# A due-time table for the planner, late decode from the first layer, and the last pair's values in another PSUM slot

## The chip, the cores and the metric

One core of one Trainium2 chip runs the whole program. The metric is the device time of one launch in microseconds (us). The kernel before took 1105.01 us, the median of three runs (1103.29, 1105.01 and 1106.9). The profiled execution, from which all rows below come, took 1104.88 us itself, of which 1103.1 us is the span that the profiler shows.

## The reference, cut to what matters

```
q, k, v: [4, 12, 448, 64]                      # batch, heads, sequence, head size
scores = q @ k.T / 8 - log(448)
x      = sigmoid(scores) @ v                    # -> [4 * 448 tokens, 768]
h      = x @ w_in                               # 768 x 2048
x      = (h - tanh(h)) @ w_out                  # 2048 x 768
gate   = sigmoid(x @ w_gate)                    # 768 x 1536
out    = (gate * (x @ w_val)) @ w_out2          # 1536 x 768
```

All of it is in float32. The kernel keeps the precision by splitting each operand into a rounded high part and a low rest and by adding three products (high with high, high with low, low with high).

## The kernel before

**Attention.** 24 head pairs p are worked one after another. For each pair TensorE makes scores `sa` and `sl` (L310, L322), ScalarE makes sigmoids `at` and `al` of them (L314, L326), and one pair later `values(p)` multiplies these with v into a PSUM tile (L338, L345), which VectorE or ScalarE copies to `x` (L353). PSUM has three slots that matter here: tag `px` holds scores (the third scores slot), tag `pv` holds the values of a pair and has one buffer. So the values of pair 23 can't begin before the copies of pair 22 have emptied `pv`.

**First layer.** 32 steps i, that is 8 groups of 256 hidden columns by 4 batches t. `hidden_mm` (L361) makes the hidden PSUM tile `ph`, a chain of ScalarE and VectorE instructions makes `h - tanh(h)` from it (`u`, `mk`, `s1`, `s2`, `y`, L395 to L434; `g` is its high part on ScalarE, L431, then its low part on VectorE, L434), and `project_group` (L468) multiplies `g` with w_out into `po`, which L481 or L585 adds to the accumulators `acc`.

**Second layer.** 12 blocks k in two passes of six (`NBLK`): a pass is one half of the batches, a block 256 of the 1536 hidden columns. A block multiplies by a Strassen scheme: seven products (`TERMS` = a11, s1, s2, a12, s3, s4, a22) with the gate weights n = 3k, then seven with the value weights n = 3k+1 (`product`, L999, into banks `pa`, `pb`, `pc`, `pe`). Copies on ScalarE (L1012) move a bank's partial sum into the next bank. `prepare` makes the operands of a pass: sums of accumulators (L629, VectorE), their highs (L762, ScalarE), their lows (L768, VectorE). `divide(n)` splits the weights: high on ScalarE (L842), lows (L853) on GpSimd, for n = 0, 1, 2 and 18 also on VectorE. `finish` makes gate times value: high `gg` on ScalarE (L1059), lows (L1064) on GpSimd, in the last block on VectorE too. The output projection of a block, 12 groups `pq` (L468), is put among the products of the next block as `fillers`, and VectorE adds each group to the output accumulator (L479, L481). Before the first block the join to layer 1 has the last groups `po31` as fillers.

**What sets the order.** All instructions are written out by a program that plans. Each piece of ScalarE, VectorE and GpSimd work is a `Task` with a due time. `spend(t, ...)` stands after each piece of TensorE work: it moves a clock `now` on by t and issues those tasks, by due time, that fit in the spare room of each engine; `must` issues one at once. Each engine and each DMA queue then works strictly in the order of issue. Fillers are placed by tables: `SHARE0` puts all 12 twelfths after s2 in block 0, `SHARE` spreads them over s2, a12, s3, s4 and a22 of the gate half, and `SHARE_END` puts those of block 5 into its value half. Operands of the second pass are planned from block 5 on (`prepare(1)`). The late decode of packed weights (`mq`: ScalarE L145, VectorE L148 to L163, written out by SyncE's queue and read back as `mm`) is planned when layer 1 has been issued.

## Time and profile before

| what | value |
|---|---|
| median of three runs | 1105.01 us |
| profiled execution, own time | 1104.88 us |
| its span | 1103.1 us |
| TensorE (PE) busy | 1084.3 us, 98% of the span, 6085 matmuls |
| VectorE (DVE) busy | 809.3 us, 73% |
| ScalarE (ACT) busy | 617.7 us, 56% |
| GpSimd (POOL) busy | 427.4 us, 39% |
| chain that ended last | PE 93%, DVE 3%, ACT 2%, POOL 1%, issue 1% |

The busy time of TensorE includes stretches at a lower clock, where each matmul takes longer. The granted clock (PEclk) stands at 1.00 in most stretches; where it stands below, a part of the stretch ran at the lower of the two levels (1.2 instead of 2.4 GHz). An instruction's idle time in square brackets is the time that its engine waited just before it, with what ended the wait.

### The profile page before, as it was taken

The numbers are of one execution on the slowest core, as the hardware profiler recorded it, in microseconds if no ns is written. First come the engines' busy times: TensorE is split into PE (matmuls) and PEld (weight loads), VectorE is DVE, ScalarE is ACT, GpSimd is POOL, SyncE is SP. The second block draws the span as 40 slices with busy tenths as digits, with TensorE's granted clock in tenths as the row PEclk, the third lists the DMA queues.
The fourth block names the chain that finished last, engine by engine and source line by source line (L and its number), as shares of the span: only waits on it lengthen the run. The fifth ranks groups of instructions, "written<-read, shape, count | busy, mean of one in ns | idle before, by whom it ended". The sixth has DMA issues, their size and how long they took to land.

```text
span 1103.1 us, 15973 instructions
## 1 busy us (share of the span) xinstructions
PE 1084.3 (98%) x6085; PEld 974.2 (88%) x6085; DVE 809.3 (73%) x1112; ACT 617.7 (56%) x861; POOL 427.4 (39%) x432
## 2 busy tenths in 40 slices
PE   9999989999999999999999999999998999999998
PEld 6677779999999999999998889999997999999997
DVE  4778647899998989899977879996669453443334
ACT  6878745577777777777767444444354334333320
POOL 5455300011111111111136357586598445546531
PEclk9999999999999999999999899999999999999999
DMA  7666302324343434244320136455212311201202
GB/s 202 191 189 188 122 1 86 101 89 128 100 143 100 144 100 141 87 129 133 113 72 29 58 132 224 159 187 172 88 42 70 136 68 58 83 32 58 87 1 100
DMA packets 40205, 119.80 MB, mean 109 GB/s; under 512 B 6080, under 2 KB 21440, under 8 KB 40128
## 3 DMA queue, kind: packets, MB, share of 16 engines
q1 hardware_dynamic: 36896, 116.38, 32.8%
q0 software_dynamic: 3072, 2.17, 0.9%
q8 instruction: 48, 0.79, 0.3%
q10 hardware_dynamic: 160, 0.23, 0.1%
q14 instruction: 29, 0.24, 0.1%
HBM read 99.09 MB, written 19.66 MB: 108 GB/s over the span
## 4 chain that ended last, share of the span: by engine, by line
PE 93%; DVE 3%; ACT 2%; POOL 1%; issue 1%; DMA 0%; SPq 0%; ACTq 0%; POOLq 0%
PE ph L361 21%; PE po L468 21%; PE pq L468 15%; PE pa L999 8%; PE pc L999 7%; PE pb L999 7%; PE pv L345 5%; PE sa L310 4%; PE pe L999 3%; PE sl L322 1%; PE pv L338 1%; DMA st<-in_w_in_dram 0%; PE pz L1173 0%; ACT at L314 0%; POOL gg L1064 0%
## 5 line engine op out<-in xcount | busy, mean ns | idle before, releaser
L468 PE MATMUL po<-g,w 128*128 128x448 f32 x1152 | 240.0, 366 | 2.1 <-ACT g L431 1.6
L361 PE MATMUL ph<-x,w 128*128 128x448 f32 x1152 | 235.8, 362 | 0.2 <-ACT at L314 0.2
L468 PEld LDWEIGHTS po<-g,w 128*128 128x128 f32 x1152 | 216.0, 189 | 21.0 <-ACT g L431 1.9
L361 PEld LDWEIGHTS ph<-x,w 128*128 128x128 f32 x1152 | 215.8, 187 | 15.3 <-ACT at L314 0.6
L178 POOL TENSOR_TENSOR w<-m,w 128x384 fp32r<-128x384 f32 x64 | 63.6, 1016 | 380.9 <-issue 299.0
L468 PE MATMUL pq<-gg,w 128*128 128x448 f32 x864 | 184.4, 364 | 5.1 <-POOL gg L1064 3.5
L468 PEld LDWEIGHTS pq<-gg,w 128*128 128x128 f32 x864 | 162.5, 188 | 17.8 <-POOL gg L1064 4.5
L853 POOL TENSOR_TENSOR w_t<-mm,w_t 128x384 fp32r<-128x384 f32 x90 | 96.8, 1105 | 137.9 <-ACT w_t L842 137.5
L481 DVE TENSOR_TENSOR acco<-pq,acco 128x448 f32<-128x448 f32 x120 | 73.8, 620 | 71.5 <-PE pq L468 70.6
L999 PE MATMUL pa<-a,w_b 128*128 128x448 f32 x432 | 94.6, 363 | 0.0
L999 PEld LDWEIGHTS pa<-a,w_b 128*128 128x128 f32 x432 | 81.5, 189 | 5.6
L314 ACT ACTIVATE at<-sa,bias_s 128x896 f32<-128x896 f32 x72 | 67.3, 1008 | 8.1 <-PE sa L310 8.0
L481 DVE TENSOR_TENSOR acc<-po,acc 128x448 f32<-128x448 f32 x90 | 55.4, 617 | 14.0 <-PE po L468 13.9
L853 POOL TENSOR_TENSOR w_b<-mm,w_b 128x384 fp32r<-128x384 f32 x54 | 59.8, 1128 | 15.0 <-ACT w_b L842 13.3
L1064 POOL TENSOR_TENSOR gg<-sg,gg 128x448 fp32r<-128x448 f32 x42 | 55.1, 1341 | 24.4 <-ACT gg L1059 24.4
L398 ACT ACTIVATE y<-ph 128x896 f32<-128x896 f32 x32 | 29.4, 919 | 59.2 <-PE ph L361 59.0
L345 PE MATMUL pv<-at,vt 128*64 128x224 f32 x576 | 60.8, 361 | 0.0
L145 ACT ACTIVATE m<-st 128x768 f32<-128x768 f32 x32 | 29.0, 908 | 56.5 <-POOL w L178 55.0
L345 PEld LDWEIGHTS pv<-at,vt 128*64 128x64 f32 x576 | 39.8, 139 | 19.7 <-issue 8.3
L842 ACT ACTIVATE w_t<-mm 128x768 fp32r<-128x768 f32 x48 | 39.3, 838 | 30.0 <-DVE mm L879 26.9
L853 POOL TENSOR_TENSOR w<-mm,w 128x384 fp32r<-128x384 f32 x44 | 47.1, 1094 | 21.3 <-ACT w L842 20.7
L310 PE MATMUL sa<-sp 64*128 64x448 f32 x432 | 51.1, 376 | 0.2 <-ACT at L314 0.2
(113 smaller groups left out, 1858.8 us busy)
## 6 DMA issues: line engine op xcount, KB each, us to landing
mm<-kept SPq DMA_DIRECT2D x36, 768.0 KB, 4.2
st<-in_w_out_dram SPq DMA_DIRECT2D x28, 768.0 KB, 4.9
st<-in_w_in_dram SPq DMA_DIRECT2D x16, 768.0 KB, 4.3
st<-in_w_gate_dram SPq DMA_DIRECT2D x12, 768.0 KB, 5.0
st<-in_w_val_dram SPq DMA_DIRECT2D x12, 768.0 KB, 4.9
kept<-mk SPq DMA_DIRECT2D x22, 384.0 KB, 5.6
kt<-in_k_dram SPq DMA_DIRECT2D x48, 112.0 KB, 3.8
kept<-mq SPq DMA_DIRECT2D x14, 384.0 KB, 5.5
```

Of the source, the lines that this page charges most:

```text
L178: (low or nc.gpsimd).tensor_tensor(out=w1[:, r], in0=mf[:, r], in1=w0[:, r].bitcast(F32), op=ALU.subtract)
L310: nc.tensor.matmul(pa[:, j, :S], kk[r, ki, c], qq[r, qi], start=(i == 0), stop=(i == 2),)
L314: nc.scalar.activation(out=at[:, :, c], in_=pa[:, :, :S], func=AF.Sigmoid, bias=bias_s, scale=qk_scale,)
L345: nc.tensor.matmul(po[j * D:(j + 1) * D, h, :SH], vt[:, j, c], at[:, j, c, h * SH:(h + 1) * SH], start=False, stop=(c == NCH - 2),)
L361: nc.tensor.matmul(o, w(i), xv(j), start=first and n == 0, stop=last and n == 2, skip_group_check=seeded,)
L398: nc.scalar.activation(out=y, in_=h, func=AF.Tanh)
L468: nc.tensor.matmul(po[:, :S], w[:, a, d], gt[:, c, j], start=n == 0 and not seeded, stop=n == last, skip_group_check=seeded,)
L481: nc.vector.tensor_tensor(out=at[:, d], in0=po[:, :S], in1=at[:, d], op=ALU.add)
L842: nc.scalar.activation(out=w0, in_=quarters(lo, hi), func=AF.Copy)
L853: eng.tensor_tensor(out=w1[:, r], in0=quarters(lo, hi)[:, r], in1=w0[:, r].bitcast(F32), op=ALU.subtract,)
L999: nc.tensor.matmul(bank[term], w[:, i, half * KH + c], t[:, j, c], start=fresh and at == 0, stop=at == 3 * KH - 1, skip_group_check=not fresh,
L1064: eng.tensor_tensor(out=gt[t][:, 1, j], in0=sg[t][:, j], in1=gt[t][:, 0, j].bitcast(F32), op=ALU.subtract,)
```

## The change

It does these things. A table `TUNE` gives an offset in us to the due time of each task. It also holds the arguments of some `spend` calls (`e0` to `e9`), a slightly smaller spare (1.94 for 2.0), flags `v{n}` and `u{k}` that let the lows of weights n and of block k's gates go to VectorE as well as to GpSimd, and for each block a plan `f{k}`: how many fillers stand after each of its 14 products. Operands of the second pass are planned from block 4 on (`early`), not from block 5, and all sums of that pass may begin at once then. The late decode is registered inside the first layer, at its step `TAIL2` = 28. The values of the last pair go to tag `px`. In the attention's last steps the first instructions of layer 1's chain for step 0 are issued in another order, and its last ones after `values(23)`. The matmuls are the same in number; the lines of the changed kernel are 36 to 42 higher than those of before.

```
+TUNE = {
+    "c28": 11.1, "c29": 1.4, "c30": -5.1, "d20": -2.4, "d21": 2.2, "d22": 6.6, "d23": 3.4,
...
+    "f0": [0, 0, 4, 0, 0, 0, 2, 0, 0, 0, 0, 0, 0, 0],
...
-        po = psx.tile([128, 2, 512], F32, tag="pv", name=f"pv{p}")
+        po = psx.tile(
+            [128, 2, 512], F32, tag="px" if p == NP - 1 else "pv", name=f"pv{p}"
+        )
...
-            spend(1.2)
+            spend(1.2, TUNE.get("e4", 0.9), TUNE.get("e5", 1.0))
...
-    SPARE = 2.0
+    SPARE = TUNE.get("spare", 2.0)
...
             self.haste = False
+            due += TUNE.get(name, 0.0)
...
-            kinds = dict(v=0.6, g=1.3) if FLEX or n in (0, 1, 2, 18) else dict(g=1.3)
+            kinds = dict(v=0.6, g=1.3) if TUNE.get(f"v{n}", n in (0, 1, 2, 18)) else dict(g=1.3)
...
-                task.add(dict(v=0.7, g=1.4) if FLEX or k == NK - 1 else dict(g=1.4), f, [h])
+                task.add(dict(v=0.7, g=1.4) if TUNE.get(f"u{k}", k == NK - 1) else dict(g=1.4), f, [h])
...
-        for term in TERMS:
+        plan = TUNE.get(f"f{k}", PLAN_END if k == NBLK - 1 else PLAN0 if k == 0 else PLAN)
+
+        def fill(at):
+            for _ in range(plan[at]):
+                if fillers:
+                    fillers.pop(0)()
+
+        for at, term in enumerate(TERMS):
             product(3 * k, term)
             gate(term)
-            if not after:
-                fill(share.get(term, 0))
+            fill(at)
...
-                run(act)
-                for f in dve[:3]:
+                for f in (act[1], act[0], act[2], dve[0], dve[1]):
                     f()
...
+            first = NPRE - len(early) // 4
+            late_u.append(NU1 + first)
+            st_at[NU1 + first] = 0.0
+            for j in range(first, NPRE):
+                decoding(j, min(begin_of(j // 2) - 16.0, begin_of(3 * NBLK - 3)))
...
-            if k == NBLK - 1:
+            if k == TUNE.get("early", NBLK - 2):
                 for term in TERMS:
                     x_free.setdefault((1, term), None)
-                x_free[1, "a11"] = 0.0
-                for term in ("s1", "s2", "s3", "s4"):
-                    x_free[1, "sum" + term] = 0.0
+                x_free[1, "a11"] = x_free[1, "sums1"] = x_free[1, "sums2"] = 0.0
+                x_free[1, "sums4"] = x_free[1, "sums3"] = 0.0
                 prepare(1, begin_of(3 * NBLK) - 4.0, free1)
```

Of the flags, `u11` is false, so the last block's gate lows, which could go to VectorE, now go to GpSimd alone: VectorE and GpSimd had two each, and now GpSimd has all four. Counted over the program, 26 lows of weights and 14 lows of gates move from GpSimd to VectorE (28 to 54 and 2 to 16). Between the first block and the fifth (blocks 1 to 4) VectorE gets 14 instructions more.

ScalarE at the join of layer 1 to block 0, before (`s2_0` is the high of the operand s2 of pass 0, `room` the copy of bank `pe`, `g31` the high of the last step of layer 1):

```order
L585 ACTIVATE acc2_2224<-po30_5_5761 128x448
L407 ACTIVATE s231_5705<-mk31_5703,gb_92 128x896
L1012 ACTIVATE pb0_5787<-pa0_5786 128x448
L762 ACTIVATE s2_0_5812<-acc0_1996 128x1344
L1012 ACTIVATE room_5783<-pe0_5789 128x448
L762 ACTIVATE s4_0_5831<-acc1_2110 128x1344
L1012 ACTIVATE pc0_5788<-pb0_5787 128x448
L431 ACTIVATE g31_5700<-y31_5702 128x896
```

The same place on ScalarE in the changed kernel:

```order
L623 ACTIVATE acc2_2224<-po30_5_5764 128x448
L1054 ACTIVATE pb0_5790<-pa0_5789 128x448
L445 ACTIVATE s231_5709<-mk31_5707,gb_92 128x896
L1054 ACTIVATE room_5786<-pe0_5792 128x448
L801 ACTIVATE s2_0_5822<-acc0_1996 128x1344
L801 ACTIVATE a22_0_5838<-acc1_2110 128x1344
L1054 ACTIVATE pc0_5791<-pb0_5790 128x448
L469 ACTIVATE g31_5704<-y31_5706 128x896
```

The copies out of `pa0` and `pe0` now stand ahead of `s2_0`, and a22's high in the place of s4's.

VectorE at the same join, before (`ph31` and `y31` are the chain of the last step of layer 1):

```order
L418 SCALAR_TENSOR_TENSOR ph31_5647<-s131_5704,ph31_5647 128x2x448
L423 SCALAR_TENSOR_TENSOR ph31_5647<-s231_5705,ph31_5647 128x2x448
L768 TENSOR_TENSOR s2_0_5812<-acc0_1996,s2_0_5812 128x448 x3
L428 COPY_PREDICATED y31_5702<-mk31_5703,ph31_5647 128x896
L629 TENSOR_TENSOR acc0_1996<-acc1_2110,acc0_1996 128x448 x2
L434 TENSOR_TENSOR g31_5700<-y31_5702,g31_5700 128x896
```

And in the changed kernel (`mq` and `st54` are the late decode):

```order
L456 SCALAR_TENSOR_TENSOR ph31_5651<-s131_5708,ph31_5651 128x2x448
L193 SCALAR_TENSOR_TENSOR mq_5462<-st54_5346,mq_5462 128x768
L199 SCALAR_TENSOR_TENSOR mq_5462<-st54_5346,mq_5462 128x768
L807 TENSOR_TENSOR s2_0_5822<-acc0_1996,s2_0_5822 128x448 x3
L461 SCALAR_TENSOR_TENSOR ph31_5651<-s231_5709,ph31_5651 128x2x448
L466 COPY_PREDICATED y31_5706<-mk31_5707,ph31_5651 128x896
L472 TENSOR_TENSOR g31_5704<-y31_5706,g31_5704 128x896
```

Two decode instructions come in ahead of s2's lows, the chain's step L423 moves behind these lows, and the sums L629 leave the place between the chain's last two steps.

ScalarE where the second pass begins (block 6), before (`gg5_0` and `gg5_1` are the gate highs of block 5, of which block 6's fillers need the lows; `p56_0` is the copy of bank `pe`):

```order
L842 ACTIVATE w17_0_7690<-mm17_7591 128x768
L762 ACTIVATE s4_1_7726<-acc3_2346 128x1344
L762 ACTIVATE a22_1_7738<-acc3_2346 128x1344
L762 ACTIVATE s3_1_7750<-acc2_2224 128x1344
L842 ACTIVATE w17_1_7776<-mm17_7591 128x768
L1012 ACTIVATE pb6_7761<-pa6_7760 128x448
L1059 ACTIVATE gg5_0_7416<-sg5_0_7414 128x896
L1059 ACTIVATE gg5_1_7417<-sg5_1_7415 128x896
L1012 ACTIVATE p56_0_7759<-pe6_7763 128x448
```

And in the changed kernel:

```order
L881 ACTIVATE w17_0_7698<-mm17_7591 128x768
L801 ACTIVATE a22_1_7724<-acc3_2346 128x1344
L1101 ACTIVATE gg5_0_7425<-sg5_0_7423 128x896
L881 ACTIVATE w17_1_7748<-mm17_7591 128x768
L881 ACTIVATE w19_b1_7753<-mm19_7713 128x768
L1054 ACTIVATE pb6_7762<-pa6_7761 128x448
L801 ACTIVATE s4_1_7791<-acc3_2346 128x1344
L1054 ACTIVATE p56_0_7760<-pe6_7764 128x448
L801 ACTIVATE s3_1_7804<-acc2_2224 128x1344
```

`gg5_0` moves ahead of the copy of `pa6`, and the highs of s4 and s3 move behind it. On TensorE the fillers of block 5 stand behind the product a12 of block 6 (4 after a12, 1 after s3, 5 after s4, 1 each after s1 and a12 of the value half), where before two stood behind s2 and two behind a12.

## Rows read from the trace of the kernel before

**Rows 1.** The page's first part: busy time, share of the span, instructions.

```profile
PE 1084.3 (98%) x6085; PEld 974.2 (88%) x6085; DVE 809.3 (73%) x1112; ACT 617.7 (56%) x861; POOL 427.4 (39%) x432
```

**Rows 2.** Stretches: length, busy of PE, PEld, DVE, ACT, POOL; PEclk, DMA, GB/s.

```profile
132.00:152.00 20.00, 16.93 (x123) 12.26 (x120) 9.38 (x10) 10.11 (x13) 1.99 (x2) 0.91 0.12 41
...
592.00:615.00 23.00, 20.04 (x80) 16.42 (x79) 20.24 (x23) 15.76 (x21) 14.17 (x11) 0.85 0.21 69
...
660.00:810.00 150.00, 150.00 (x751) 140.59 (x751) 117.51 (x151) 65.58 (x99) 105.21 (x86) 1.00 0.47 156
...
830.00:860.00 30.00, 25.38 (x116) 22.68 (x116) 26.95 (x36) 11.64 (x15) 19.87 (x16) 0.94 0.24 84
```

**Rows 3.** Timeline of PE, attention's end: start, length, operation, [idle before].

```profile
141.50 0.61 PE L338 MATMUL pv<-al,vt 64*64 64x224 f32 x8
142.04 2.49 PE L345 MATMUL pv<-at,vt 128*64 128x224 f32 x24
147.41 1.02 PE L338 MATMUL pv<-al,vt 64*64 64x224 f32 x8 [2.88 <-DVE x L353]
148.36 3.55 PE L345 MATMUL pv<-at,vt 128*64 128x224 f32 x24
```

**Rows 4.** Timeline of ACT, the last reader of the px slot.

```profile
134.82 0.64 ACT L326 ACTIVATE al<-sl,bias_s 128x448 f32<-128x448 f32 x1
```

**Rows 5.** Timeline of PE, join of layer 1 to block 0.

```profile
601.76 1.97 PE L999 MATMUL pe<-s,w_t 128*128 128x448 f32 x9
...
606.51 0.47 PE L999 MATMUL pb<-s,w_t 128*128 128x448 f32 x1 [0.80 <-DVE s L768]
608.58 3.86 PE L468 MATMUL po<-g,w 128*128 128x448 f32 x8 [1.60 <-ACT g L431]
...
646.12 2.08 PE L468 MATMUL pq<-gg,w 128*128 128x448 f32 x9 [1.12 <-DVE w L853]
```

**Rows 6.** Timeline of ACT, the same join.

```profile
602.46 1.32 ACT L762 ACTIVATE s<-acc 128x1344 fp32r<-128x1344 f32 x1
603.76 0.54 ACT L1012 ACTIVATE room<-pe 128x448 f32<-128x448 f32 x1
...
607.58 0.95 ACT L431 ACTIVATE g<-y 128x896 fp32r<-128x896 f32 x1
```

**Rows 7.** Timeline of DVE, the same join.

```profile
602.01 1.10 DVE L423 SCALAR_TENSOR_TENSOR ph<-s,ph 128x896 f32<-128x896 f32 x1
603.81 2.65 DVE L768 TENSOR_TENSOR s<-acc,s 128x448 fp32r<-128x448 f32 x3 [0.70 <-ACT s L762]
606.38 1.17 DVE L428 COPY_PREDICATED y<-mk,ph 128x896 f32<-128x896 int32 x1
...
609.45 1.08 DVE L434 TENSOR_TENSOR g<-y,g 128x896 fp32r<-128x896 f32 x1
```

**Rows 8.** Timeline of PE, start of the second pass.

```profile
843.96 2.08 PE L999 MATMUL pb<-s,w_t 128*128 128x448 f32 x9 [1.78 <-ACT pb L1012]
...
848.68 0.47 PE L468 MATMUL pq<-gg,w 128*128 128x448 f32 x1 [1.85 <-POOL gg L1064]
850.15 2.88 PE L468 MATMUL pq<-gg,w 128*128 128x448 f32 x7 [0.99 <-POOL gg L1064]
```

**Rows 9.** Timeline of PE, then of POOL, the last block's projection.

```profile
1085.45 0.88 PE L468 MATMUL pq<-gg,w 128*128 128x448 f32 x3 [0.61 <-POOL gg L1064]
...
1083.86 3.04 POOL L1064 TENSOR_TENSOR gg<-sg,gg 128x448 fp32r<-128x448 f32 x2 [12.27 <-ACT gg L1059]
```

**Rows 10.** Timeline of DVE (three rows), then of POOL beside the last two.

```profile
617.64 0.54 DVE L853 TENSOR_TENSOR w_b<-mm,w_b 128x384 fp32r<-128x384 f32 x1
...
782.03 0.62 DVE L481 TENSOR_TENSOR acco<-pq,acco 128x448 f32<-128x448 f32 x1 [0.26 <-PE pq L468]
782.58 1.38 DVE L853 TENSOR_TENSOR w_b<-mm,w_b 128x384 fp32r<-128x384 f32 x1
...
781.55 1.99 POOL L853 TENSOR_TENSOR w_b<-mm,w_b 128x384 fp32r<-128x384 f32 x2
```

More of the change, by code (lines that the diff above doesn't have):

```diff
@@ L29 @@
 GGAP = 24
+TUNE = {
[32 rows of a table added]
+}
 @with_exitstack
@@ L1004, in product @@
                     at += 1
-            spend(1.8, 0.2 if term == "s3" else 0.9, 0.4 if term in ("a11", "s2") else 0.8)
+            spend(
+                1.8, TUNE.get("e0", 0.2) if term == "s3" else TUNE.get("e1", 0.9),
+                TUNE.get("e2", 0.4) if term in ("a11", "s2") else TUNE.get("e3", 0.8),
+            )
             if LAST.get(term) == key:
@@ L1088, in value @@
                 finish(1, join(sg[1][:, 0], pc, sg[1][:, 0], ALU.mult))
-        share = SHARE0 if k == 0 else SHARE
-        after = SHARE_END if k == NBLK - 1 else {}
-        total = len(fillers)
-        def fill(part):
-            while len(fillers) > total - total * part // 12:
-                fillers.pop(0)()
-        for term in TERMS:
+        plan = TUNE.get(f"f{k}", PLAN_END if k == NBLK - 1 else PLAN0 if k == 0 else PLAN)
[4 more added lines that the diff above has]
+        for at, term in enumerate(TERMS):
             product(3 * k, term)
             gate(term)
-            if not after:
-                fill(share.get(term, 0))
+            fill(at)
         if k:
             p5.append(mp[0].tile([128, S], F32, tag="p5", name=f"p5{k}_1"))
-        for term in TERMS:
+        for at, term in enumerate(TERMS):
             product(3 * k + 1, term)
@@ L1109, in block @@
             value(term)
-            fill(after.get(term, 0))
+            fill(7 + at)
+        while fillers:
+            fillers.pop(0)()
         g_t["b", k] = gt
-    SHARE0 = dict(s2=12)
-    SHARE = dict(s2=2, a12=4, s3=7, s4=10, a22=12)
-    SHARE_END = dict(a11=2, s1=4, s2=6, a12=8, s3=10, s4=12)
+    PLAN0 = [0, 0, 6] + [0] * 11
+    PLAN = [0, 0, 2, 2, 3, 3, 2] + [0] * 7
+    PLAN_END = [0] * 7 + [2] * 6 + [0]
     g_task = {}
@@ L1141, in run @@
                         box["po"] = seed(f"pq{k}_{t}_{d + 1}", at, d + 1)
-                    spend(1.2)
+                    spend(1.2, TUNE.get("e6", 0.9), TUNE.get("e7", 1.0))
                     if by_act and d % 2:
@@ L1206 @@
         assert not todo
-        for f in dve[3:]:
+        for f in (act[3], act[4], dve[2], dve[3], dve[4]):
             f()
         values(NP - 1)
+        for f in dve[5:]:
+            f()
         att_ctx.close()
@@ L1254 @@
                 busy["v"] = max(busy["v"], now[0])
-                spend(7.2)
+                spend(7.2, TUNE.get("e8", 0.9), TUNE.get("e9", 1.0))
                 if i > TAIL2:
@@ L1284 @@
         last_chain.append(chain)
-        first = NPRE - len(early) // 4
-        late_u.append(NU1 + first)
-        st_at[NU1 + first] = 0.0
-        for j in range(first, NPRE):
-            decoding(j, min(begin_of(j // 2) - 16.0, begin_of(3 * NBLK - 3)))
         fillers = list(groups1(N1 - 1))
```

30 rows, old and new, of the table TUNE are left out of this document.

## The prediction, made before the changed kernel ran

> **What bounds the kernel now.** I read the page's first part, then the stretches, then in the stretches that lose time the timeline of TensorE, and from each of its waits the timeline of the engine named there. The first shows TensorE busy for 1084.3 of 1103.1 us [rows 1]. The stretches tell what busy means: from 660 to 810 us it ran 751 matmuls in 150.00 us, 0.200 us each, at a clock of 1.00 [rows 2]. That is the floor, and the matmuls are the same in number after the change; only time over 0.200 us a matmul can go. By this price the stretch 592 to 615 loses 23.0 - 80 x 0.2 = 7.0 us and the stretch 830 to 860 loses 30.0 - 116 x 0.2 = 6.8 us, both at a mean granted clock under 1.00 [rows 2]. So a wait there costs twice: its own length, and matmuls at 1.2 GHz in place of 2.4 GHz behind it. The end of attention, 132 to 152, is the third such stretch [rows 2].
>
> **Place 1, the last pair's values in the px slot.** TensorE waits 2.88 us ahead of the values of pair 23, until VectorE has emptied the slot of pair 22. These values then take from 147.41 to 151.91 = 4.50 us, the same work for pair 22 from 141.50 to 144.53 = 3.03 us [rows 3]: the wait has left the clock low. The px slot was last read at 134.82 + 0.64 = 135.46 [rows 4], six us before it is wanted now. The values of pair 23 would then begin at 144.53, at the high clock, and end at 147.56, not 151.91: **-4.35**. What could be late next is the chain of layer 1's step 0, since the copies out of pair 23's slot stand ahead of its last instructions now; but those copies move up by the same 4 us. I take no cost, and up to +1 for a new wait there.
>
> **Place 2, the join of layer 1 to block 0.** Before, ScalarE makes the high of s2 at 602.46 and copies bank pe afterwards [rows 6]. Now the copy stands first, and pe's matmuls end at 601.76 + 1.97 = 603.73 [rows 5]. So the copy runs from 603.75 to 604.3, the high takes 1.32 to 605.6 [rows 6], and VectorE's three lows 2.65 to 608.2 [rows 7]. The two decode instructions ahead of these lows cost nothing: no row here has them, but at the 1.10 of the nearest VectorE row [rows 7] they need 2.2 us, and VectorE has from 603.1 until 605.6. Behind the lows now come the chain's step L423 (1.10), L428 (1.17), ScalarE's g (0.95) and VectorE's low of g (1.08) [rows 6, 7]: 608.2 + 4.3 = 612.5, less some 0.1 of overlap at each of the joints. Before, that low ended at 609.45 + 1.08 = 610.53 [rows 7]. The sums that stood between the last two steps are gone, which is in this count. That is +1.9. If GpSimd is idle then, the three lows take about 0.54 each, as the one low without a neighbour did [rows 10], not 0.88, and +0.9 is left; I take +1.5. TensorE's wait of 1.12 for a weight low at 646.12 [rows 5] goes, since weights 2 and 3 may now be split by either engine and the plan brings no fillers before s2: -1.1. Sum of the place **+0.4**, with bounds of -3 (the waits of 0.80 and 1.60 us [rows 5] and half the clock loss go) and +3 (none of the 1.1 comes, and the longer wait keeps the clock low for another 1.5).
>
> **Place 3, start of the second pass.** TensorE waits 1.78 us for the copy of pa, then 1.85 and 0.99 for the lows of block 5's gates [rows 8], and the rest of the 6.8 is low clock. Three things change. Sums and a high for the second pass are made in block 4 already. The copy no longer waits behind three highs of 1.3 each, but behind one, a gate high of 0.95 and two weight highs; how much earlier it starts depends on when those weights have landed, so I keep the 1.78 whole. And gate 0's high stands ahead of the copy, its lows may go to VectorE, and the product a12 stands ahead of the first filler, which gives the lows 9 x 0.2 = 1.8 us more. The two waits for gates, 2.84 in sum, should go, and with them the low clock: 6.8 - 1.8 = **-5.0**. Bounds: -6.8, if the copy is early too, and 0, if VectorE is as late with the lows as GpSimd.
>
> **What the lows on VectorE cost.** 40 lows move to VectorE. A low with nothing beside it on GpSimd takes 0.54 us, one beside GpSimd 1.38 [rows 10]. At 1.38, 14 instructions more in the steady stretch bring VectorE from 117.51 to 136.8 of 150 us [rows 2]: it still fits, and TensorE, busy for the whole of that stretch, hides it. I take 0; if the cover goes, see the third rival.
>
> The Trainium skill, "SBUF — State Buffer", section "Who interferes with whom", says that a VectorE instruction with two inputs in SBUF and a GpSimd instruction take a shared pair of ports in turn, and that one with at most one SBUF input does not contend. The trace agrees on both sides: 1.38 against 0.54 for the low, which has two such inputs, and 0.62 for the evacuation L481 beside GpSimd, which reads one operand from PSUM [rows 10]. By this rule moving a low wins no throughput, only a place in another queue, so it bears on the second rival, and it speaks against the third.
>
> **Tail.** The last block's gate 0 had one low on VectorE and one on GpSimd; now GpSimd has both, ahead of both of gate 1. GpSimd took 3.04 us for two [rows 9], so the second ends at 1083.86 + 3.04 = 1086.90, and the sixth matmul, which ran at 1085.45 + 0.2 = 1085.65 [rows 9], waits for it: **+1.3**. Bounds 0 (VectorE was running beside GpSimd, without it GpSimd may take half) and +1.5.
>
> **Other edits.** The fill plans, the offsets and the decode in the first layer move work that stands beside a TensorE which loses nothing: 150.00 of 150.00 us in the long stretch of layer 2 [rows 2]. I take 0, from -0.5 (less DMA crowding) to +3 (one new wait of 1.5 with its clock).
>
> **Sum.** -4.35 + 0.4 - 5.0 + 1.3 = -7.65 against the profiled execution's own 1104.88 (its span of 1103.1 and 1.8 around it): 1097.2. The median of the three runs is 1105.01, 0.1 from it, so I forecast 1097.
>
> **Rivals.**
> 1. *Clean recovery.* At place 3 the copy is early as well (-6.8), the tail costs nothing, and place 2 loses only the 1.1: 1104.9 - 4.35 - 6.8 - 1.1 = 1092.6. For it: ScalarE is half idle, with 65.58 busy of 150 in the steady stretch, so an early copy is a matter of order alone [rows 2]. Against it: at place 2 the order moves the s2 high later.
> 2. *Gains given back on the port.* Lows on VectorE at 1.38 keep TensorE waiting at places 2 and 3 as GpSimd did: 2.84 of wait and the low clock stay, and only place 1 with the tail's cost, less some of the 1.1, is won: 1104.9 - 4.35 + 1.3 - 0.5 = 1101.3. For it: VectorE is at 26.95 of 30 us in 830 to 860 [rows 2]. Against it: the order of ScalarE there changes apart from the port.
> 3. *VectorE's queue becomes the bound, and the kernel slower.* VectorE works in order, so each moved low stands ahead of an evacuation of the output projection. A low and an evacuation take 1.38 + 0.62 = 2.0 us [rows 10], while TensorE makes a group of six matmuls in 1.2: 0.8 late, when no free bank takes it up. With half of the 40 lows badly placed that is 16 us: 1097 + 16 = 1113. It decides from some 10 lows on, which eat up the 7.65. For it: VectorE is the fullest engine beside TensorE. Against it: 0.00 lost in 150 us with 117.51 busy [rows 2].
> 4. *The slot is not free.* Another tile or a due time holds the px slot, or the chain of step 0 makes TensorE wait as long: place 1 wins nothing, the rest stays: 1104.9 + 0.4 - 5.0 + 1.3 = 1101.6. Against it: the 135.46 above.
>
> **How the numbers follow.** A run of this kernel tells from no change what is over 0.3%, 3.3 us: faster is under 1101.7, slower over 1108.3. Forecast 0.50 (its own range 1093.5 to 1100.5), clean recovery 0.21, port 0.15, slower 0.08, slot 0.06. Faster: 0.49 + 0.21 + about two thirds of the 0.21 of rivals 2 and 4 = 0.83; same: the other third and a little of the forecast's tail, 0.10; slower 0.07. The range leaves out the slower rival and the lower end of clean recovery: 1090.5 to 1102.5.
>
> **What would show it.** Place 1: no wait ahead of pair 23's values, and layer 1 beginning behind them about 4.4 us earlier. Place 2: g's low of the last step about 1.5 us later against the start of block 0, and no wait for weight 2's low. Place 3: in the first product of block 6 a wait of 1.8 or less for the copy, none for the gates, clock 1.00. Tail: a wait of some 1.3 more in the last block's first group. It is wrong if VectorE's busy share in blocks 1 to 4 nears 150 of 150 with waits of TensorE for evacuations, or if new waits stand in the blocks where none were.

## The result and the profile after

The changed kernel takes **1092.88 us** (median of 4 runs, 1092.74 to 1094.55), against 1104.95 for the kernel before on the same chip: a ratio of 0.989, with a 95% interval of 0.9875 to 0.9912. The profiled execution took 1092.74 us with a span of 1091.0, so 12.1 us went out of the span. 1097 was forecast, with a range of 1090.5 to 1102.5.

First the same views as [rows 1] and [rows 2]: the page's first part, and the stretches (length, busy time of PE, PEld, DVE, ACT and POOL with their instructions, PEclk, DMA share, GB/s).

```profile
PE 1078.5 (99%) x6085; PEld 971.6 (89%) x6085; DVE 822.6 (75%) x1153; ACT 617.8 (57%) x861; POOL 384.9 (35%) x391
```

```profile
132.00:152.00 20.00, 19.81 (x143) 15.76 (x142) 9.88 (x11) 10.73 (x13) 1.99 (x2) 1.00 0.12 41
...
592.00:615.00 23.00, 18.29 (x80) 15.54 (x79) 19.10 (x26) 14.25 (x18) 10.62 (x9) 0.93 0.34 117
...
660.00:810.00 150.00, 150.00 (x752) 140.61 (x750) 119.46 (x162) 64.85 (x99) 84.94 (x69) 1.00 0.44 140
...
830.00:860.00 30.00, 30.00 (x151) 28.12 (x150) 26.25 (x36) 13.19 (x20) 22.73 (x18) 1.00 0.35 128
```

TensorE runs the same 6085 matmuls and is busy 5.8 us less, because fewer of them run at the low clock. The first and the last stretch now hold 143 and 151 matmuls where 123 and 116 stood. The join, 592 to 615, still holds 80. VectorE did not fill up: 119.46 of 150 us, 2 us more than before with 11 instructions more.

Where the time came from is read from the start of the same product in both traces. Each row gives how much earlier it starts now, and the difference to the row ahead.

| product | earlier by, us | step, us | what stands there |
|---|---|---|---|
| layer 1, next matmul behind pair 23's values | 4.45 | -4.45 | place 1 |
| block 0, a11 | 4.73 | -0.28 | a ScalarE wait of 0.21 in layer 1 gone |
| block 0, a11 of the value half | 4.03 | +0.70 | the join |
| behind block 1's fillers | 5.43 | -1.40 | wait for weight 2's low |
| block 6, a11 | 5.61 | -0.18 | in block 5 a product of 1.98 us where 1.80 is usual gone |
| block 6, s3 of the gate half | 12.64 | -7.03 | place 3 |
| end | 12.10 | +0.54 | tail |

**Place 1.** TensorE at the end of attention (start, length, operation; a wait would stand in brackets):

```profile
144.97 2.49 PE L383 MATMUL pv<-at,vt 128*64 128x224 f32 x24
147.39 5.88 PE L399 MATMUL ph<-x,w 128*128 128x448 f32 x28
```

The 2.88 us ahead of pair 23's values [rows 3] are gone, its 24 matmuls take 2.49, as pair 22's did before [rows 3], and layer 1 follows at 147.39 without a wait.

**Place 2.** At the join TensorE waits longer than before, 1.84 and 2.73 us against 0.80 and 1.60 [rows 5]:

```profile
595.23 1.96 PE L1038 MATMUL pa<-a,w_b 128*128 128x448 f32 x9
...
600.83 2.21 PE L1038 MATMUL pb<-s,w_t 128*128 128x448 f32 x9 [1.84 <-ACT s L801]
605.77 6.97 PE L506 MATMUL po<-g,w 128*128 128x448 f32 x24 [2.73 <-ACT g L469]
612.58 1.96 PE L1038 MATMUL pa<-a,w_b 128*128 128x448 f32 x9
```

ScalarE and VectorE there, to be set against [rows 6] and [rows 7]:

```profile
599.02 0.54 ACT L1054 ACTIVATE room<-pe 128x448 f32<-128x448 f32 x1 [0.26 <-PE pe L1038]
...
604.76 0.95 ACT L469 ACTIVATE g<-y 128x896 fp32r<-128x896 f32 x1 [1.16 <-DVE y L466]
```

```profile
600.81 1.70 DVE L807 TENSOR_TENSOR s<-acc,s 128x448 fp32r<-128x448 f32 x3 [1.79 <-ACT s L801]
...
605.75 1.09 DVE L472 TENSOR_TENSOR g<-y,g 128x896 fp32r<-128x896 f32 x1 [1.02 <-ACT g L469]
```

The order is the one that the prediction went through: copy, high, three lows, then the chain to g. The three lows take 1.70 us, not 2.65. For the same stretch the trace of before has, on TensorE:

```profile
599.96 1.96 PE L999 MATMUL pa<-a,w_b 128*128 128x448 f32 x9
...
608.58 10.61 PE L468 MATMUL po<-g,w 128*128 128x448 f32 x36 [1.60 <-ACT g L431]
619.03 1.96 PE L999 MATMUL pa<-a,w_b 128*128 128x448 f32 x9
```

Before, 27 + 36 = 63 matmuls took 619.03 - 599.96 = 19.07 us; at 0.2 each that is 12.6, and 6.47 are lost, 2.40 of them in waits and 4.07 to the low clock. Now 27 + 24 = 51 take 612.58 - 595.23 = 17.35 us, and 7.15 are lost, 4.57 in waits and 2.58 to the clock. (The other 12 matmuls run later. What is put down to the clock holds, at each wait, also the 0.16 us or so in which the matmul ahead of it ends: nine matmuls in a row take 1.96 us by the rows, and the next begins 1.80 after their start.) So the waits grew by 2.17 and the join by 0.7.

The longer of the two waits is for ScalarE's high of g, before and after. Counted from the start of block 0, that high ended at 607.58 + 0.95 - 599.96 = 8.57 us before [rows 6], and ends at 604.76 + 0.95 - 595.23 = 10.48 now, 1.91 later.

**Weight 2's low.** The wait of 1.12 us in block 1 [rows 5] is gone. ScalarE makes weight 2's two highs in the changed kernel ahead of block 1, where before the second of them came 4.4 us into it (block 1 begins at 634.80 now and began at 638.83). The line of before stands first:

```profile
643.27 0.84 ACT L842 ACTIVATE w<-mm 128x768 fp32r<-128x768 f32 x1
...
630.68 1.56 ACT L881 ACTIVATE w<-mm 128x768 fp32r<-128x768 f32 x2
```

**Place 3.** TensorE, ScalarE and GpSimd at the start of the second pass, to be set against [rows 8]:

```profile
836.40 1.96 PE L1038 MATMUL pb<-s,w_t 128*128 128x448 f32 x9
838.20 1.96 PE L1038 MATMUL pa<-a,w_b 128*128 128x448 f32 x9
840.00 4.96 PE L506 MATMUL pq<-gg,w 128*128 128x448 f32 x24
```

```profile
831.36 0.95 ACT L1101 ACTIVATE gg<-sg 128x896 fp32r<-128x896 f32 x1 [1.22 <-DVE sg L1070]
...
834.80 0.53 ACT L1054 ACTIVATE pb<-pa 128x448 f32<-128x448 f32 x1 [1.02 <-PE pa L1038]
```

```profile
833.72 1.47 POOL L667 TENSOR_TENSOR acc<-acc 128x448 f32<-128x448 f32 x1
835.15 2.97 POOL L1106 TENSOR_TENSOR gg<-sg,gg 128x448 fp32r<-128x448 f32 x2
```

The three waits are gone. ScalarE stood idle for 1.02 us until TensorE had ended pa, and then made the copy at once. The high of gate 0 was made 3.4 us ahead of that copy, and its two lows, still on GpSimd, end at 835.15 + 2.97 = 838.12, ahead of the fillers at 840.00.

**Tail.** TensorE in the last block's projection, to be set against [rows 9]:

```profile
1072.43 0.47 PE L506 MATMUL pq<-gg,w 128*128 128x448 f32 x1 [0.22 <-POOL gg L1106]
1073.52 13.68 PE L506 MATMUL pq<-gg,w 128*128 128x448 f32 x67 [0.62 <-POOL gg L1106]
```

GpSimd now makes all four lows, and takes 4.47 us for the four:

```profile
1071.22 4.47 POOL L1106 TENSOR_TENSOR gg<-sg,gg 128x448 fp32r<-128x448 f32 x4 [13.26 <-ACT gg L1101]
```

That is 1.12 each, and TensorE waits 0.22 and then 0.62 us for them, where it waited 0.61 before.

### The profile page after: what moved, and what is told of

Read it like the earlier page. It is cut to its first block, busy times and chain, and to the rows that moved or that the text cites. A ratio compares the mean times of both kernels' runs of the same rounds, so it can differ in the third digit from the quotient of the medians.

```text
span 1091.0 us, 15944 instructions
## 1 busy us (share of the span) xinstructions
PE 1078.5 (99%) x6085; PEld 971.6 (89%) x6085; DVE 822.6 (75%) x1153; ACT 617.8 (57%) x861; POOL 384.9 (35%) x391
## 3 DMA queue, kind: packets, MB, share of 16 engines
q0 software_dynamic: 3072, 2.17, 0.9%
## 4 chain that ended last, share of the span: by engine, by line
PE 96%; ACT 1%; DMA 1%; DVE 1%; POOL 0%; issue 0%; SPq 0%; ACTq 0%; DVEq 0%; POOLq 0%
PE ph L399 21%; PE po L506 21%; PE pq L506 16%; PE pa L1038 8%; PE pc L1038 8%; PE pb L1038 8%; PE pv L383 5%; PE pe L1038 4%; PE sa L346 4%; PE sl L358 1%; PE pv L376 1%; DMA st<-in_w_in_dram 0%; ACT at L350 0%; DMA kt<-in_k_dram 0%; POOL gg L1106 0%
## 5 line engine op out<-in xcount | busy, mean ns | idle before, releaser
L399 PEld LDWEIGHTS ph<-x,w 128*128 128x128 f32 x1152 | 215.8, 187 | 15.3 <-ACT at L350 0.6
L892 POOL TENSOR_TENSOR w_t<-mm,w_t 128x384 fp32r<-128x384 f32 x72 | 79.9, 1131 | 141.6 <-ACT w_t L881 137.8
L892 POOL TENSOR_TENSOR w_b<-mm,w_b 128x384 fp32r<-128x384 f32 x54 | 63.6, 1198 | 38.9 <-ACT w_b L881 36.7
L1106 POOL TENSOR_TENSOR gg<-sg,gg 128x448 fp32r<-128x448 f32 x30 | 39.7, 1347 | 31.3 <-ACT gg L1101 31.1
L346 PEld LDWEIGHTS sa<-sp 64*128 64x128 f32 x432 | 38.5, 184 | 12.2 <-issue 7.3
```

The source lines that it names most:

```text
L346: nc.tensor.matmul(pa[:, j, :S], kk[r, ki, c], qq[r, qi], start=(i == 0), stop=(i == 2),)
L399: nc.tensor.matmul(o, w(i), xv(j), start=first and n == 0, stop=last and n == 2, skip_group_check=seeded,)
L892: eng.tensor_tensor(out=w1[:, r], in0=quarters(lo, hi)[:, r], in1=w0[:, r].bitcast(F32), op=ALU.subtract,)
L1106: eng.tensor_tensor(out=gt[t][:, 1, j], in0=sg[t][:, j], in1=gt[t][:, 0, j].bitcast(F32), op=ALU.subtract,)
```

## The experiments

All are timed against the kernel before. Twelve kernels ran. The theory was that three places hold the gain, each won by an order: a free slot at place 1, and at place 3 the gate's high ahead of the copy with its lows in a queue that is free. The rivals to it were that the flags' work sharing, the earlier sums or the fill plans win the time, or that the parts don't add up place by place.

**px_only: place 1 alone.** The kernel before, with one line changed:

```
-        po = psx.tile([128, 2, 512], F32, tag="pv", name=f"pv{p}")
+        po = psx.tile([128, 2, 512], F32, tag="px" if p == NP - 1 else "pv", name=f"pv{p}")
```

> The kernel before with one edit: the values of pair 23 go to the px slot. Theory (place 1 stands alone): no wait ahead of pair 23's values, the clock stays at 1.00 from 132 to 152 us, 4.4 us less, 1100.5 us. Rival (the slot or layer 1's chain holds TensorE instead): a new wait at the same place, 1104 to 1105 us.

Measured: 1100.83 us, ratio 0.9963 (0.9948 to 0.9978); the median is 4.2 us lower, and the span 1103.1 - 1099.0 = 4.1. Its stretch at the end of attention (columns as in [rows 2]):

```profile
132.00:152.00 20.00, 19.81 (x144) 15.77 (x142) 9.70 (x11) 10.51 (x13) 1.98 (x2) 1.00 0.12 41
```

It is the changed kernel's stretch, and the later waits are those of before: 1.78, 1.86 and 0.99 us at place 3. The next matmul of layer 1 starts 151.84 - 147.56 = 4.28 us earlier. So the slot gives place 1's gain by itself.

**no_px: the change without it.**

```
-            [128, 2, 512], F32, tag="px" if p == NP - 1 else "pv", name=f"pv{p}"
+            [128, 2, 512], F32, tag="pv", name=f"pv{p}"
```

> The changed kernel with the values of pair 23 back in the pv slot. Theory: the wait of 2.9 us ahead of pair 23's values comes back, and with it the low clock, 4.4 us more: 1097.3 us; places 2 and 3 as in the changed kernel. Rival (the gains of the places aren't additive, later work absorbs the wait): 1093 to 1094 us.

Measured: 1095.26 us, ratio 0.9916 (0.9894 to 0.9937). The loss, 2.4 us, is about half of what was expected. TensorE at the same place:

```profile
146.23 0.61 PE L376 MATMUL pv<-al,vt 64*64 64x224 f32 x8 [1.51 <-DVE x L391]
146.77 2.49 PE L383 MATMUL pv<-at,vt 128*64 128x224 f32 x24
```

The wait is 1.51 us and not 2.88, and the values behind it run at the high clock. The other order of layer 1's chain there had shortened the wait by itself: VectorE's copy out of pair 22's slot begins at 145.56, 0.84 us behind the end of that pair's values, and before it began at 146.73, 2.20 behind it. At the next matmul of layer 1 the slot alone is worth 4.28 us (px_only), the other edits alone 151.84 - 149.19 = 2.65, and both 4.45: the gains of two edits at one place don't add. Block 0 begins 1.71 us later than in the changed kernel. (The rest of its 3.3 us more of span lies in the tail, on which see the last section.)

**no_offsets: the change without the due-time offsets.**

```
-            due += TUNE.get(name, 0.0)
+            due += 0.0
```

> The changed kernel with all due-time offsets taken as zero; the fill plans, the flags, the px slot, the early second pass and the early decode stay. Theory (the offsets carry place 3, since without them three operand highs stand ahead of block 5's gate high on ScalarE again): 3 to 7 us of place 3 come back, 1096 to 1100 us. Rival (flags and fill plans carry it): 1092 to 1094 us.

Measured: 1099.53 us, ratio 0.9952 (0.9937 to 0.9967), 6.65 more than the change. TensorE at place 3:

```profile
842.50 1.48 PE L1038 MATMUL pb<-s,w_t 128*128 128x448 f32 x6 [2.16 <-DVE w_t L892]
...
847.35 4.61 PE L506 MATMUL pq<-gg,w 128*128 128x448 f32 x20 [0.76 <-DVE gg L1106]
```

Of the 7.00 us more of span, 4.76 are lost at the start of block 6; 1.74 are lost ahead of block 0, mostly at the start of attention, and 0.59 in block 2. So the offsets carry place 3, but not in the way that was expected. The three operand highs do stand ahead of the gate's high again, and it still ends 11 us ahead of the first filler (833.54 + 0.93 against 845.62). What TensorE waits for is a weight's high (0.64 us), that weight's lows (2.16) and the gate's lows (0.76), which stand behind eight weight lows on VectorE. What the offsets order at place 3 is the whole row of highs and lows in front of it, not the gate alone.

**flags_before: the change without the flags.** Which lows may go to VectorE is as before; offsets and plans stay.

```
-            kinds = dict(v=0.6, g=1.3) if TUNE.get(f"v{n}", n in (0, 1, 2, 18)) else dict(g=1.3)
+            kinds = dict(v=0.6, g=1.3) if n in (0, 1, 2, 18) else dict(g=1.3)
...
-                task.add(dict(v=0.7, g=1.4) if TUNE.get(f"u{k}", k == NK - 1) else dict(g=1.4), f, [h])
+                task.add(dict(v=0.7, g=1.4) if k == NK - 1 else dict(g=1.4), f, [h])
```

> The changed kernel with the flags of before: lows of weights 0, 1, 2 and 18 and of the last block's gates may go to VectorE, all others to GpSimd alone; offsets and plans stay. Theory (the lows on VectorE win no throughput, the order does; without them GpSimd has some 40 lows more and the planner puts the three operand highs ahead of block 6's copy again): 2 to 5 us more from waits at block 6 and block 1, 1095 to 1098 us, tail 0.5 us less. Rival (the port shared by VectorE and GpSimd makes it equal where the lows run): 1092 to 1093.5 us.

Measured: 1102.47 us, ratio 0.9987 (0.9974 to 1.0). 9.6 of the 12.1 us are gone, more than either side expected, and the tail is as in the changed kernel, not 0.5 shorter. TensorE's waits (us in total, times, longest):

```profile
PE pq L506 <- POOL gg L1106: 6.2, 8, 1.2
```

and GpSimd in block 2, with TensorE's wait for it:

```profile
678.77 6.50 POOL L1106 TENSOR_TENSOR gg<-sg,gg 128x448 fp32r<-128x448 f32 x4
```

```profile
682.50 0.47 PE L506 MATMUL pq<-gg,w 128*128 128x448 f32 x1 [1.18 <-POOL gg L1106]
```

Two of the eight waits are the tail's, as in the changed kernel. Six stand in blocks 2, 6 and 7, where the changed kernel has none (the kernel before has some in block 6 alone). By the starts of the products 2.66 us are lost in block 2, 1.34 in block 3 (a wait of 0.94 for a copy), 2.01 in block 6, 2.42 in block 7 and 0.40 in block 8; 0.55 are lost ahead of block 0. Four gate lows in a row are 6.5 us of GpSimd. The offsets and plans are made for lows on two engines; that they set the queue of GpSimd alone too late is read from this order, and no run had offsets made for it.

The three operand highs stand ahead of block 6's copy again, as was expected, but TensorE does not wait for that copy. ScalarE, first before the change and then here:

```profile
838.64 1.33 ACT L762 ACTIVATE s<-acc 128x1344 fp32r<-128x1344 f32 x1 [4.06 <-DVE acc L629]
...
834.31 1.34 ACT L801 ACTIVATE s<-acc 128x1344 fp32r<-128x1344 f32 x1 [1.94 <-DVE acc L667]
```

Before, the first of the highs began 0.23 us behind the start of block 6 (838.41), after ScalarE had stood idle for a sum of VectorE's; here it begins 3.03 us ahead of it (837.34). For the copy it counts when the highs begin, and not only how many of them stand ahead.

**flags_only: the flags without offsets and plans.** The table holds the 32 flags only, and the early sums are in block 5 as before.

```
-    "c28": 11.1, "c29": 1.4, "c30": -5.1, "d20": -2.4, ... "early": 4,
-    "f0": [0, 0, 4, 0, 0, 0, 2, 0, 0, 0, 0, 0, 0, 0],
...
+    "early": 5, "u0": True, "u1": True, ... "v35": True, "v5": True, "v8": False,
```

> The changed kernel with the table cut to the 32 flags that let lows of weights and gates go to VectorE: no due offsets, the fill plans, spend arguments and spare of before, the second pass planned from block 5 on as before; the px slot and the early decode stay. Theory (the flags free GpSimd, and the planner then puts block 5's gate high ahead of block 6's copy by itself): place 1 won, 4.1 us, and most of place 3, 5 to 7 us; 1093.5 to 1096.5 us. Rival (flags and offsets gain only together, as the run without flags says of the offsets): the waits for gates at block 6 stay, 1099 to 1102 us.

Measured: 1100.06 us, ratio 0.9954 (0.9937 to 0.9971); less than 1 us better than px_only. VectorE and TensorE at place 3:

```profile
836.56 3.06 DVE L668 TENSOR_TENSOR acc<-acc,acc 128x448 f32<-128x448 f32 x2
...
841.15 2.10 DVE L1107 TENSOR_TENSOR gg<-sg,gg 128x448 fp32r<-128x448 f32 x2
```

```profile
841.82 0.74 PE L507 MATMUL pq<-gg,w 128*128 128x448 f32 x1 [2.99 <-DVE gg L1107]
```

The gate's high is early here too and the wait for the copy is gone. But the lows, now on VectorE, stand behind 3.06 us of sums and the operand lows that follow them, and TensorE waits 2.99. From the start of block 6 to its product s3 this kernel takes 6.88 us more than the changed one. A flag opens a second queue; the offsets choose the place in it. Beside the slot (px_only, 1100.83) the flags alone are worth 0.8 us, the offsets and plans alone (flags_before) cost 1.6, and flags and plans without offsets (no_offsets) are worth 1.3; together they are worth 1100.83 - 1092.88 = 8 us. (These kernels have the early decode and the other order in attention too, which px_only lacks.)

**gg_late: gate 0 of block 5 made ready 6 us later in the planner.** This is to undo place 3's order alone; the planner then places what follows anew.

```
-                (), lambda: ready,
+                (), lambda: ready + (6.0 if (k, t) == (NBLK - 1, 0) else 0.0),
```

> The changed kernel, planned with the high of block 5's first gate (gg5_0) held back 6 us, so that on ScalarE it stands behind three copies of block 6; the fill plans, flags and offsets stay. Theory (what removed the waits for gates at the second pass's start is the early place of that high on ScalarE): a wait of 1 to 3 us for its lows at block 6's first fillers and low clock behind it, 2 to 5 us more, 1095 to 1098 us. Rival (sums of the second pass made in block 4, or the product a12 ahead of the fillers, removed it): 1092.5 to 1094 us.

Measured: 1100.19 us, ratio 0.9954 (0.9936 to 0.9971). TensorE, then VectorE, at place 3:

```profile
841.47 1.08 PE L506 MATMUL pq<-gg,w 128*128 128x448 f32 x4 [1.03 <-ACT gg L1101]
843.12 0.47 PE L506 MATMUL pq<-gg,w 128*128 128x448 f32 x1 [0.57 <-POOL gg L1106]
845.48 4.79 PE L506 MATMUL pq<-gg,w 128*128 128x448 f32 x15 [1.88 <-DVE gg L1106]
```

```profile
838.62 6.27 DVE L807 TENSOR_TENSOR s<-acc,s 128x448 fp32r<-128x448 f32 x5
844.81 0.61 DVE L1106 TENSOR_TENSOR gg<-sg,gg 128x448 fp32r<-128x448 f32 x1
```

One due time costs 7.3 us (6.7 in the span of the profile). 5.82 of these are lost between the start of block 6 and its s3, of the 7.03 that place 3 had won: 1.03 + 0.57 + 1.88 = 3.48 of waits, and the rest is for the most part low clock (granted 0.94 in 830 to 860). The mechanism is as expected, and the time 2 us above the range that was given, since a low on VectorE then stands behind five operand lows. No wait for the copy came back.

**f6_before: block 6's old fill plan.** Fillers behind s2 again, ahead of a12.

```
-    "f6": [0, 0, 0, 4, 1, 5, 0, 0, 1, 0, 1, 0, 0, 0],
+    "f6": [0, 0, 2, 2, 3, 3, 2, 0, 0, 0, 0, 0, 0, 0],
```

> The changed kernel with block 6's fill plan as before: two fillers already after s2, ahead of the product a12, the rest as in the table of before. Theory (the gate's lows end at 838.1 in the changed kernel's trace, where these fillers would begin at 838.2): no or a very short wait, under 1 us more, 1092.5 to 1094 us. Rival (the 1.8 us that a12 gives the lows are needed, as the prediction counted): a wait of 1 us and more with the low clock, 1094.5 to 1097 us.

Measured: 1093.03 us, ratio 0.9894 (0.9875 to 0.9913): no change. TensorE:

```profile
837.23 1.96 PE L1038 MATMUL pb<-s,w_t 128*128 128x448 f32 x9
839.03 2.56 PE L506 MATMUL pq<-gg,w 128*128 128x448 f32 x12
```

The fillers stand right behind s2, and nothing waits. GpSimd there:

```profile
835.99 2.98 POOL L1106 TENSOR_TENSOR gg<-sg,gg 128x448 fp32r<-128x448 f32 x2
```

The two lows end at 838.97, 0.06 us ahead of the first filler. So the 1.8 us that a12 gives the lows, a step of the prediction, were not needed, but nothing was to spare.

**early5: the early sums in block 5 as before.** `"early": 4` becomes `"early": 5`.

> The changed kernel with the second pass planned from block 5 on, as before, and all else as changed. Theory (the order of ScalarE at block 6 is the same in both): 1092.5 to 1094 us. Rival (the sums made in block 4 are what clears place 3): a wait of 1.5 us and more at block 6, 1094.5 to 1098 us.

Measured: 1093.82 us, ratio 0.99 (0.9885 to 0.9915), no new wait. The sums made in block 4 are not what clears place 3.

**decode_late: the late decode begun after layer 1, as before.**

```
-            first = NPRE - len(early) // 4
-            late_u.append(NU1 + first)
...
+        first = NPRE - len(early) // 4
+        late_u.append(NU1 + first)
```

> The changed kernel with the late decode registered after layer 1, as before the change. Theory (it is work beside a TensorE that never waits for it; block 6's order on ScalarE is the same): no difference, 1092.5 to 1094 us, though one decode instruction more stands on ScalarE ahead of block 0's first copy. Rival (the early start frees VectorE and GpSimd in block 0, so lows of block 0 or 1 come late without it): 1095 us and more, with waits in blocks 0 to 2.

Measured: 1094.23 us, ratio 0.9911 (0.9894 to 0.9928). The join costs the same; one wait of 0.61 us comes in block 5, for a weight's low on GpSimd, about 1 us in the trace. At this size the times don't tell it from nothing (the runs of the two overlap).

**u11: the last block's lows free to go to VectorE.** `"u11": False` becomes `True`.

> The changed kernel with the last block's gate lows allowed on VectorE again. Theory: at the tail the wait of 0.62 us for GpSimd's second low goes and 0.22 with it or less, 0.5 us less, 1092.4 us. Rival (the two engines slow each other as much as they share): 1092.9 us. The trace decides, since the difference is near the spread of the times.

Measured: 1093.76 us, ratio 0.9895 (0.9877 to 0.9913). GpSimd at the tail:

```profile
1071.33 4.44 POOL L1106 TENSOR_TENSOR gg<-sg,gg 128x448 fp32r<-128x448 f32 x4 [13.25 <-ACT gg L1101]
```

Nothing moved: the four lows stay on GpSimd, and the time is the changed kernel's within the spread of the runs. That the flag forbids VectorE is not the whole cause: with the flag set, the planner still chooses GpSimd. In its code a task that may go to either goes to GpSimd when it can end there ahead of its due time by more than the spare, and the offsets of this block's gates (15.3 and 8.5 us) set that late; with both at -10 and the flag set (join2, below) VectorE makes three of the four. A miss, and it corrects the reading of the diff that the prediction had.

**join: the last chain steps ahead of s2's lows.** The longer waits at the join were, with the tail, what the change loses. This kernel issues the chain up to its end there first.

```
+        while i == N1 - 2 and chain.at <= te:
+            chain.go(chain.start())
...
+            if k == 0 and term == "a11":
+                op_task[0, "s2"].flush()
+            if k == 0 and term == "s1":
+                last_chain[0].go(last_chain[0].start())
```

> The changed kernel with another order at the join of layer 1 to block 0 only: layer 1's last chain is issued up to its copy step before block 0, s2's high and lows right behind the first copy, g31's high right behind the room copy. Theory (the 4.6 us of waits and the low clock behind them that are left at the join come from the order on ScalarE and VectorE, not from the length of the chain): po31 starts some 4 us earlier after block 0's first product, waits under 1.5 us, 5 to 6.5 us less, 1086.5 to 1088 us. Rival (the chain's own length sets it, and other work moved behind it makes TensorE wait later): 1091 to 1094 us.

Measured: 1095.91 us, ratio 0.992 (0.9905 to 0.9935), slower than the change. The join itself gave 5.15 us. TensorE behind it:

```profile
614.11 0.47 PE L1040 MATMUL pb<-s,w_b 128*128 128x448 f32 x1 [0.88 <-POOL s L809]
615.91 0.47 PE L1040 MATMUL pb<-s,w_b 128*128 128x448 f32 x1 [1.33 <-POOL s L809]
...
636.41 1.48 PE L1040 MATMUL pe<-s,w_t 128*128 128x448 f32 x6 [0.81 <-POOL w_t L894]
639.95 1.48 PE L1040 MATMUL pb<-s,w_t 128*128 128x448 f32 x6 [1.45 <-POOL w_t L894]
```

TensorE came 5 us earlier to operands and weights whose due times had not moved, and waited there: 2.21 us for operand lows, then 2.26 for weight lows, and smaller losses further on. The gain was given back, and more.

**join2: the same with the offsets of what comes next.** The chain is issued up to an earlier point, the rest of it behind s1, and seven offsets of the table move: operands of pass 0, weight 1 and the last block's gates.

```
-    "w1": 4.9, "xa22_0": -6.6, "xs2_0": 6.5, "xs3_0": 8.2, "xs4_0": 18.5,
+    "w1": 0.9, "xa22_0": 0.0, "xs2_0": 0.0, "xs3_0": 4.0, "xs4_0": 14.0,
-    "g11_0": 15.3, "g11_1": 8.5, "u11": False,
+    "g11_0": -10.0, "g11_1": -10.0, "u11": True,
...
+        while i == N1 - 2 and chain.at <= t4:
+            chain.go(chain.start())
...
+            if k == 0 and term == "s1":
+                while last_chain[0].at <= 10:
+                    last_chain[0].go(last_chain[0].start())
```

> The changed kernel with the join's order as in the run before it (layer 1's last chain issued up to its fourth step before block 0, g31's high right behind the room copy, s2's high ahead of it by its due time), with five due offsets of block 0 (a22, s2, s3, s4, weights 1) chosen so that the order of ScalarE, VectorE and GpSimd after the join is nearly that of the changed kernel, and the last block's gate lows allowed on VectorE with an early due time. Theory (the first join kernel won 5 us at the join and lost them to lows that its replanning put late, not to the join's order): the 5 us stay, no new wait over 0.5 us in blocks 0 to 6, tail 1 us less, 1086 to 1088 us. Rival (VectorE and GpSimd have no room behind the join, whatever the order): waits of 2 us and more come back in blocks 0 and 1, 1090 to 1093 us.

Measured: **1089.49 us** (1089.05 to 1091.02), ratio 0.9867 (0.9852 to 0.9881), the fastest of all, 3.4 below the change; all four runs lie below all four of the change, though the two intervals touch. Its TensorE:

```profile
614.96 2.07 PE L1040 MATMUL pc<-a,w_t 128*128 128x448 f32 x9 [1.40 <-DVE room L1072]
...
637.00 1.48 PE L1040 MATMUL pb<-s,w_t 128*128 128x448 f32 x6 [0.77 <-POOL w_t L894]
...
1069.29 14.90 PE L506 MATMUL pq<-gg,w 128*128 128x448 f32 x72 [0.56 <-ACT gg L1103]
```

Of 5.4 us won at the join, the two new waits and smaller losses behind them leave 1.9; the tail gives 1.1, since VectorE now makes three of its lows and GpSimd one. It stays above the 1086 to 1088 that were expected, by these waits.

## Why the prediction held, step by step

The time, 1092.88, lies within the whole range, but below the forecast's own 1093.5 to 1100.5: the forecast was 4 us short, and the range held because it took in most of the first rival.

- **Place 1, forecast -4.35, measured -4.45.** Right in place, size and reason: px_only gives 4.28 by itself. The slot had been free for nine us when pair 23 wanted it (144.43), not six.
- **Place 2, the join, forecast +1.5, measured +0.70.** The order came as worked out, and g's low ended 606.84 - 595.23 = 11.61 us after block 0's start, against 610.53 - 599.96 = 10.57 before: 1.04 later. But the step priced the wrong instruction: TensorE waits for g's high on ScalarE in both traces, and that came 1.91 later. The waits grew by 4.57 - 2.40 = 2.17 us. The term had no row for the other side, 1.49 us less of low clock. That the sum came out near is in part luck: the two errors point opposite ways. **The wait for weight 2's low, forecast -1.1, measured -1.40.** Right in size: in the trace of before, the twelve matmuls from 644.24 to 648.03 take 1.39 us more than 0.2 each, the wait with what the clock and the end of the matmul ahead add. The reason given was wrong: the flags leave weights 2 and 3 as they were (2 could go to VectorE before, 3 can't in either), and neither plan has fillers before s2. What moved is weight 2's highs on ScalarE, and with them the lows. They are as early, and the wait is gone, in no_offsets and in flags_before; in flags_only they come late and 0.32 us of the wait is left.
- **Place 3, forecast -5.0, measured -7.03.** This is the step that failed. "I keep the 1.78 whole": the copy's wait went too. The copy's only neighbours ahead of it on ScalarE were a gate high and two weight highs, and these had ended 1.02 us before TensorE had pa ready. The prediction left open when those weights land and took the term's dear end; the -6.8 of its bounds, the place's whole loss, was the better value. No single family of edits carries this: the copy's wait is gone without the offsets, without the flags, with the flags alone and with the early sums taken back; px_only has it in full (1.78), and join has 0.41 of it.
- **The reason given for the lows was wrong in two parts.** "Its lows may go to VectorE": they stayed on GpSimd. "The product a12 gives the lows 1.8 us more": f6_before takes that away at no cost, with 0.06 us to spare. What clears them is the early high on ScalarE (gg_late) and a place near the front of their queue (flags_only, where the high is as early and the lows are not).
- **Tail, forecast +1.3, measured +0.54.** GpSimd took 1.12 us a low, with no low on VectorE beside it, and not 1.52; a gain of that kind was in its lower bound. Flag and offsets each keep the lows on GpSimd: u11 takes the flag away and nothing moves.
- **Other edits, forecast 0.** Right in the sum (-0.28 and -0.18), wrong as a reason: offsets and flags are not neutral one by one. Taking one family away costs 6.65 or 9.6 us, the latter mostly in blocks 2 to 7.
- **The rivals.** Clean recovery gave 1092.6 and is what happened at place 3 and the weight's low, with the join and the tail costing 1.24 between them. Of the port rival the time did not come (1101.3), and taking the lows off VectorE makes the kernel slower (flags_before). At place 3 its mechanism was not put to the test, since the lows stayed on GpSimd there. Where they did go to VectorE, TensorE waited for them: 2.99 us in flags_only, 1.88 in gg_late, 0.76 in no_offsets, each time with other work ahead of them in VectorE's queue. The bound on that queue did not come: 150.00 of 150.00 us of TensorE with 162 VectorE instructions in it, and VectorE busy for 119.46 us and not 136.8.

Not settled: why the clock rose sooner at the join, and what made weight 2's highs early. No run takes away the fill plans as a whole, the arguments of `spend` or the other order in attention by itself, so their shares are not known.

## What to carry to other kernels

Read for each wait at a seam which engine's queue the awaited instruction stands in and what stands ahead of it; a move within a queue or to another wins whole waits, and the clock behind them, while busy shares stay the same. A second queue and a place in it are one edit: here the flags alone were worth under 1 us, the offsets and plans alone less than nothing, and all together 8. After a gain of several us at one seam, re-time everything that is due behind it, or the gain comes back as waits there.

## What the runs showed of the chip

- More waiting cost less clock: at the join 4.57 us of waits went with 2.58 us lost to the low clock, where 2.40 us had gone with 4.07. In join, waits of 0.24 to 1.45 us left the granted clock at 1.00 in 592 to 615 and in 615 to 645, and in join2 one of 1.40 did too. The price of a wait is not fixed by its length.
- Nor is it the same each time. In the tail, behind the same waits, the same 67 matmuls took 13.68 us in the changed kernel and 15.27 in u11, whose stretch 1060 to 1088 has a mean granted clock of 0.94 and not 1.00. no_px, flags_only and f6_before show the longer time too (15.28, 15.27 and 15.26). A profile's span can differ by 1.6 us through this alone.
- The mean granted clock of a stretch does not say how many matmuls ran slowly: in decode_late 592 to 615 has 0.85 and 81 matmuls, in the changed kernel 0.93 and 80. Counting the matmuls at 0.2 us is the safer reading.
- GpSimd makes a gate low in 1.12 us with no low on VectorE beside it (4.47 for four) and in 1.52 with one (3.04 for two [rows 9]). VectorE makes a low of s2 in 0.57 us with GpSimd idle for all but the last 0.4 us (1.70 for three) and in 0.88 beside it (2.65 for three [rows 7]). Either engine's instructions take longer beside the other's. Whether they run more slowly then or stand still for a part of the time the rows don't show.
